# The last 128 rows of the output leave as two column halves, over two engines and two DMA queues

## The chip, the core and the metric

The kernel runs on one core of a Trainium2 chip. The metric is the time of one execution on the device in microseconds (us). Lower is better.

## The reference

Chunked attention is followed by a two-layer feed-forward network, all in float32. The sizes are batch 4, 8 heads, 768 positions, head dimension 64; then 3072 tokens, model width 512, hidden width 2048.

```
for c in range(nc):                         # 24 chunks of 32 queries
    scores = scale * np.matmul(q_c, k_full.transpose(0, 1, 3, 2))   # 8 memory keys + up to 56 neighbours
    a = softmax(scores)
    out[:, :, c_start:c_end] = np.matmul(a, v_full)
x = out.transpose(0, 2, 1, 3).reshape(B * S, H * D)                 # 3072 x 512
h = x @ w_in                                                        # 3072 x 2048
g = np.maximum(h, 0.0) + alpha * np.minimum(h, 0.0)
return g @ w_out                                                    # 3072 x 512
```

## The kernel before, in words

The 3072 tokens are cut into 8 blocks (NBLK) of 384 tokens (BT). For each block the kernel computes the attention of four pairs of heads, and then the feed-forward network over 16 hidden pieces (NF) of 128. For one piece, `up` (L659) makes `h_ps` with 12 matmuls, ScalarE and VectorE turn it into `gh` and `gl` (L668 to L681), and `down` (L689) adds its product with the piece of `w_out` to three PSUM tiles `o_ps`, one for each 128 tokens of the block (NTT = 3). `down` goes over the three tiles in order, three matmuls each, so in the last piece tile 0 is complete first, tile 1 second and tile 2 last. The attention of later blocks is spread between the feed-forward matmuls of earlier ones; in the last block nothing of it is left.

When the last piece of a block is done, `store` (L729) takes its three tiles to HBM. For each tile there are two steps: `copy` takes `o_ps` from PSUM to a tile `o_t` in SBUF (L736 on ScalarE; in block 1 L733 on VectorE instead), and `send` issues one DMA of 256 KB (128 rows of 2 KB) from SyncE (SP, L740). All other loads are issued from SP too (L246 to L259, L448, L557). ScalarE issues no DMA.

The order of the work is not the order in which the steps are added. Every step goes into a plan (`Plan`, L106) with an engine, an estimated cost, the keys that it reads and writes, and a `rest` that says how urgent it is. `Plan.send` (L126) then plays the plan through with these costs. In each turn it takes the engine that could start earliest, and on it, of the steps that are ready, the one with most work behind it. The step is emitted at that moment, so the order in the played plan is the order in each engine's queue:

```
            engine = min(at, key=at.get)
            n = max((n for n in able if self.steps[n][0] == engine and ready[n] <= at[engine]),
                    key=lambda n: (behind[n], -n))
```

Between a step and one that depends on it on another engine, the plan counts 0.07 us (HOP); for a step of SP it counts 2.3 us (LAND). The last `down` is one step with a cost of 2.09 us for all nine matmuls, and it writes the keys of all three tiles, ("o", 0) to ("o", 2). In the played plan the three tiles are therefore complete at the same moment. On the chip the waits come from the instructions themselves, so a copy waits for the matmuls of its own tile. Waits of one engine's queue are served in the queue's order.

At the end of the program every engine meets at a barrier (L867), which comes behind SP's waits for the transfers still under way.

Of the kernel before, what the change touches and what calls it, by code (L numbers as in the profile page):

```python
# [9 lines left out]
F32 = mybir.dt.float32  # L10
# [8 lines left out]
P = 128  # L19
# [8 lines left out]
BT = 384  # L28
NBLK = B * S // BT
NT = BT // TQ  # L30
NPAIR = H // 2
DM, DF = 512, 2048
NK = DM // P
NF = DF // P
NTT = BT // P
# [24 lines left out]
PE, DVE, ACT, POOL, SP = "PE", "DVE", "ACT", "POOL", "SP"  # L60
# [102 lines left out]
def body(ctx: ExitStack, tc: tile.TileContext, qvw, kw, first, w_in, w_out, alpha, out):  # L163
    nc = tc.nc
# [12 lines left out]
    tmp = ctx.enter_context(tc.tile_pool(name="tmp", bufs=1))  # L177
# [31 lines left out]
    step = plan.add  # L209
    state, xs = {}, {}  # L210

    def rest(place):
        return (len(ORDER) - place) * PAIR
# [515 lines left out]
    def store(blk, o_ps):  # L729
        def copy(tt, t, o):  # L730
            if blk == 1:
                o["t"] = kept[tt]
                nc.vector.tensor_tensor(out=o["t"], in0=o_ps[tt], in1=o["t"], op=ALU.add)  # L733
            else:
                o["t"] = tmp.tile([P, DM], F32, name="o_t", tag=f"o{t}")
                nc.scalar.copy(out=o["t"], in_=o_ps[tt])  # L736

        def send(tt, o):
            r = blk * BT + tt * P
            nc.sync.dma_start(out=out[r:r + P, :], in_=o["t"])  # L740

        for tt in range(NTT):
            t = tt if blk == 1 else NTT + tt % 2 if blk == 0 else next(ntmp) % NTMP
            o = {}
            place = PLACE[blk, NF - 1] + 1
            step(DVE if blk == 1 else ACT, 0.68 if blk == 1 else 0.59, partial(copy, tt, t, o), reads=[("o", i) for i in range(NTT)],
                 writes=[("tmp", t)], rest=rest(place))
            step(SP, 0.75, partial(send, tt, o), reads=[("tmp", t)])
# [35 lines left out]
    o_ps = {}  # L784
    for blk, f in ORDER:
        if blk == 0:
            decode(f)
        f0, f1 = (0, NF) if blk != 1 else (0, NJOINT) if f < NJOINT else (NJOINT, NF)
        add_up, add_bend, add_down = hidden(blk, f, f0, f1 - 1)
        add_up()  # L790
        if down is not None:
            down()
        if done is not None:
            done()
            done = None
        add_bend()
        now = todo.get(PLACE[blk, f], [])
        olds, news = ([u for u, part in now if part == which] for which in (2, 0))
        if olds or news:
            attend(PLACE[blk, f], olds, news)  # L800
        for u in olds:
            split(u, "h1" if u % size(u) else "a")
            if u + 2 < NU:
                load_v(u + 2)
        for u, part in now:
            if part == 1:
                weights(u)
                turn(u)
        for u in news:
            unit_begins(u)  # L810
        o = o_ps.setdefault((blk, f1), [])
        down = partial(add_down, o)
        if f == f1 - 1:
            done = partial(keep if f1 < NF else store, blk, o)
# [56 lines left out]
```

## Time and profile before

| | |
|---|---|
| median of 3 runs | 604.88 us (604.76 to 605.04) |
| the profiled execution | 605.43 us |
| its span, first to last instruction | 603.7 us |
| busy: PE (matmul) | 596.3 us, 99% |
| busy: PEld (weight load) | 531.0 us, 88% |
| busy: DVE (VectorE) | 397.7 us, 66% |
| busy: ACT (ScalarE) | 214.1 us, 35% |
| busy: POOL (GpSimd) | 35.7 us, 6% |
| DMA, all by SP's queue but for code loading | 48.98 MB, mean 81 GB/s |

The shares are of the span. The span of 603.7 us and the 605.43 us are of one execution; 1.73 us of it lie outside the first and last instruction. An engine's busy time holds no waiting and no issuing of DMAs.

### The profile page before, as it was taken

How to read it: one execution, taken by the hardware profiler on the slowest of the kernel's cores; microseconds unless marked ns; L12 is line 12 of the kernel's file. 1: busy time of each engine (PE TensorE's matmuls, PEld its weight loads, DVE VectorE, ACT ScalarE, POOL GpSimd, SP SyncE). 2: the span in 40 equal slices, each digit the busy share in tenths (PEclk: the TensorE clock that was granted, in tenths of full speed). 3: DMA queues.
4: the chain of work that ended last, by engine and by line, in shares of the span. 5: the costliest groups of instructions: out<-in, count | busy, mean ns of one | idle time of the engine just before them, and what ended most of it. 6: DMA issues, size and time to landing. Idle time of an engine off the chain costs nothing.

```text
span 603.7 us, 11483 instructions
## 1 busy us (share of the span) xinstructions
PE 596.3 (99%) x4622; PEld 531.0 (88%) x4622; DVE 397.7 (66%) x962; ACT 214.1 (35%) x596; POOL 35.7 (6%) x61
## 2 busy tenths in 40 slices
PE   8999999999999999999999999999999999999997
PEld 4789899888989889999899998899998898999986
DVE  5788998877958677749386593847748485433331
ACT  3688878644322314232142412314132131121101
POOL 3400000001001001001010000101000010000000
PEclk9999999999999999999999999999999999999999
DMA  8999500113240303130021303103031100010001
GB/s 335 355 408 408 205 0 1 33 33 103 68 134 1 99 2 100 52 100 0 25 76 53 100 1 94 42 18 99 1 99 53 36 2 2 1 52 1 0 1 53
DMA packets 20933, 48.98 MB, mean 81 GB/s; under 512 B 2448, under 2 KB 5520, under 8 KB 20880
## 3 DMA queue, kind: packets, MB, share of 16 engines
q1 hardware_dynamic: 20880, 48.25, 22.5%
q8 instruction: 36, 0.59, 0.4%
q14 instruction: 17, 0.14, 0.1%
HBM read 41.95 MB, written 6.29 MB: 80 GB/s over the span
## 4 chain that ended last, share of the span: by engine, by line
PE 96%; DMA 2%; DVE 1%; ACT 0%; issue 0%; SPq 0%; ACTq 0%
PE h_ps L659 44%; PE o_ps L689 44%; PE a_ps L397 3%; PE s_ps L306 2%; DMA early<-first 1%; DMA w_t<-w_in 1%; PE s_ps L267 1%; PE s_ps L281 1%; PE a_ps L517 1%; DVE w_t L588 0%; PE o_ps L504 0%; DVE w_t L592 0%; DVE xl L436 0%; DVE a L596 0%; ACT a L580 0%
## 5 line engine op out<-in xcount | busy, mean ns | idle before, releaser
L659 PE MATMUL h_ps<-xh,w 128*128 128x384 f32 x1024 | 260.6, 335 | 0.3 <-DVE w L607 0.3
L689 PE MATMUL o_ps<-w,gh 128*128 128x512 f32 x768 | 238.3, 392 | 0.0
L659 PEld LDWEIGHTS h_ps<-xh,w 128*128 128x128 f32 x1024 | 185.2, 188 | 2.0 <-DVE w L607 0.6
L659 PE MATMUL h_ps<-xl,w 128*128 128x384 f32 x512 | 173.5, 339 | 0.6 <-DVE xl L436 0.6
L689 PEld LDWEIGHTS o_ps<-w,gh 128*128 128x128 f32 x768 | 144.1, 188 | 29.1
L689 PE MATMUL o_ps<-w,gl 128*128 128x512 f32 x384 | 149.7, 390 | 0.0
L668 ACT ACTIVATE g<-h_ps 128x384 f32<-128x384 f32 x128 | 63.8, 498 | 192.0 <-PE h_ps L659 187.0
L671 DVE SCALAR_TENSOR_TENSOR g<-g,rise,h_ps 128x384 f32<-128x384 f32 x128 | 78.4, 613 | 78.6 <-ACT g L668 77.2
L382 DVE STREAM_TRANSPOSE pt<-e 32x192 f32<-32x192 f32 (+1 forms) x336 | 99.4, 300 | 13.6 <-POOL e L361 8.6
L659 PEld LDWEIGHTS h_ps<-xl,w 128*128 128x128 f32 x512 | 96.1, 188 | 3.9 <-DVE xl L436 1.0
L689 PEld LDWEIGHTS o_ps<-w,gl 128*128 128x128 f32 x384 | 72.1, 188 | 14.0
L681 DVE TENSOR_TENSOR gl<-g,gh 128x384 fp32r<-128x384 f32 x128 | 72.2, 565 | 4.8 <-ACT gh L677 1.9
L361 POOL TENSOR_TENSOR e<-e,den 128x384 f32<-128x384 f32 x24 | 22.2, 924 | 436.7 <-DVE den L358 436.7
L677 DVE CAST gh<-g 128x384 fp32r<-128x384 f32 x104 | 37.8, 365 | 13.0 <-PE o_ps L689 7.5
L432 ACT CAST xh<-a_ps 128x384 fp32r<-128x384 f32 x32 | 14.4, 483 | 88.0 <-PE a_ps L397 86.0
L340 ACT ACTIVATE e<-s_ps,mx 128x64 f32<-128x64 f32 x144 | 43.0, 320 | 6.9 <-DVE mx L332 6.9
L340 ACT ACTIVATION_READ_ACCUMULATOR e<-s_ps,mx 128x1 f32 x144 | 30.9, 215 | 0.0
L365 ACT COPY e<-e 128x192 f32<-128x192 f32 x24 | 8.4, 352 | 47.0 <-DVE pt L382 41.4
L436 DVE TENSOR_TENSOR xl<-a_ps,xh 128x384 fp32r<-128x384 f32 x32 | 17.5, 549 | 10.0 <-ACT xh L432 10.0
L736 ACT COPY o_t<-o_ps 128x512 f32<-128x512 f32 x21 | 12.3, 587 | 27.3 <-PE o_ps L689 25.9
L318 DVE MEMSET s_ps<- 32x16 f32 x12 | 0.9, 72 | 30.6 <-PE s_ps L306 30.5
L397 PEld LDWEIGHTS a_ps<-pt,v_t 128*64 128x64 f32 x384 | 16.3, 137 | 4.9 <-issue 4.9
(52 smaller groups left out, 306.2 us busy)
## 6 DMA issues: line engine op xcount, KB each, us to landing
w_t<-w_in SPq DMA_DIRECT2D x16, 512.0 KB, 10.2
w_t<-w_out SPq DMA_DIRECT2D x16, 512.0 KB, 10.2
qk<-kw SPq DMA_DIRECT2D x24, 272.0 KB, 3.5
v_t<-qvw SPq DMA_DIRECT2D x24, 256.0 KB, 4.2
out<-o_t SPq DMA_DIRECT2D x24, 256.0 KB, 2.1
early<-first SPq DMA_DIRECT2D x8, 656.0 KB, 6.4
qk<-qvw SPq DMA_DIRECT2D x24, 192.0 KB, 4.3
early<-first SPq DMA_DIRECT2D x8, 256.0 KB, 6.7
```

Source lines behind the costliest of these rows:

```text
L340: nc.scalar.activation(out=st["e"][:, i], in_=st["s"][h2][:, n], func=AF.Exp, scale=SCALE, bias=d["mx"][:, u - us[0], n, h2:h2 + 1], accum ...
L361: nc.gpsimd.tensor_tensor(out=st["e"], in0=st["e"], in1=st["den"].broadcast_to([P, NJ * 2, KW]), op=ALU.mult)
L382: nc.vector.transpose(out=pts[u % NPT][quad * CH:(quad + 1) * CH, j, t0:t0 + n1 - n0].rearrange("p t h q -> p (t h) q"), in_=(st["e"], zer ...
L397: nc.tensor.matmul(out=st["a"][h2 * D:(h2 + 1) * D, t * TQ:(t + 1) * TQ], lhsT=st["v"][:, t, h2, :], rhs=pts[u % NPT][:, :, t, h2, :], sta ...
L432: nc.scalar.copy(out=st["xh"], in_=st["a"][:, :BT])
L436: nc.vector.tensor_tensor(out=xl, in0=st["a"][:, :BT], in1=st["xh"].bitcast(F32), op=ALU.subtract)
L659: nc.tensor.matmul(out=h["ps"][:, :BT], lhsT=ws[f, 0][:, wk, k * P:(k + 1) * P], rhs=xs[first + k][xk], start=(k == 0 and n == 0), stop=(k ...
L668: nc.scalar.activation(out=h["g"], in_=h["ps"][:, :BT], func=AF.Relu, scale=-1.0)
L671: nc.vector.scalar_tensor_tensor(out=h["g"], in0=h["g"], scalar=rise[:, f:f + 1], in1=h["ps"][:, :BT], op0=ALU.mult, op1=ALU.add)
L677: copy(out=h["gh"], in_=h["g"])
L681: nc.vector.tensor_tensor(out=h["gl"], in0=h["g"], in1=h["gh"].bitcast(F32), op=ALU.subtract)
L689: nc.tensor.matmul(out=o_ps[tt], lhsT=h[gk][:, tt * P:(tt + 1) * P], rhs=ws[f, 1][:, wk], start=(f == first_f and i == 0), stop=(f == last ...
```

## The change

For the last tile of the last block, `copy` and `send` are replaced by two pairs of steps. VectorE copies columns 0 to 255, and SP sends them. ScalarE copies columns 256 to 511, and ScalarE itself sends them. The tile in SBUF has the shape [128, 2, 256]. The plan is told a cost of 0.35 us for each copy and 0.4 us for each send. The other 23 tiles are treated as before.

```diff
+        def half(tt, t, o, i):
+            cols = slice(i * DM // 2, (i + 1) * DM // 2)
+            if not i:
+                o["t"] = tmp.tile([P, 2, DM // 2], F32, name="o_t", tag=f"o{t}")
+            copy = (nc.vector.tensor_copy, nc.scalar.copy)[i]
+            copy(out=o["t"][:, i], in_=o_ps[tt][:, cols])
+
+        def send_half(tt, o, i):
+            r = blk * BT + tt * P
+            (nc.sync, nc.scalar)[i].dma_start(out=out[r:r + P, i * DM // 2:(i + 1) * DM // 2], in_=o["t"][:, i])
+
         for tt in range(NTT):
             t = tt if blk == 1 else NTT + tt % 2 if blk == 0 else next(ntmp) % NTMP
             o = {}
             place = PLACE[blk, NF - 1] + 1
+            if (blk, tt) == (NBLK - 1, NTT - 1):
+
+                for i in range(2):
+                    step((DVE, ACT)[i], 0.35, partial(half, tt, t, o, i), reads=[("o", tt)], writes=[("tmp", t, i)], rest=rest(place))
+                    step((SP, ACT)[i], 0.4, partial(send_half, tt, o, i), reads=[("tmp", t, i)])
+                continue
             step(DVE if blk == 1 else ACT, 0.68 if blk == 1 else 0.59, partial(copy, tt, t, o), reads=[("o", i) for i in range(NTT)],
                  writes=[("tmp", t)], rest=rest(place))
             step(SP, 0.75, partial(send, tt, o), reads=[("tmp", t)])
```

## Rows read from the trace of the kernel before

**Rows 1.** The page, part 1: busy time (share of the span) and instructions

```profile
PE 596.3 (99%) x4622; PEld 531.0 (88%) x4622; DVE 397.7 (66%) x962; ACT 214.1 (35%) x596; POOL 35.7 (6%) x61
```

**Rows 2.** The chain that ended last, from 598 us: start, duration, what

```profile
597.96 1.60 PE o_ps L689 x7
...
599.62 0.59 ACT o_t L736
```

**Rows 3.** Timeline of ScalarE, the three last copies one by one: start, duration

```profile
598.22 0.59 ACT L736 COPY o_t<-o_ps 128x512 f32<-128x512 f32 x1 [6.35 <-PE o_ps L689]
...
598.90 0.59 ACT L736 COPY o_t<-o_ps 128x512 f32<-128x512 f32 x1
...
599.62 0.59 ACT L736 COPY o_t<-o_ps 128x512 f32<-128x512 f32 x1
```

**Rows 4.** Timeline of SP, the three last sends one by one

```profile
598.83 0.33 SPq L740 DMA_DIRECT2D out<-o_t  x1
...
599.51 0.33 SPq L740 DMA_DIRECT2D out<-o_t  x1
...
600.24 0.33 SPq L740 DMA_DIRECT2D out<-o_t  x1
```

**Rows 5.** The tail by windows: engines' busy time, then PEclk, DMA share, GB/s

```profile
core 0: us, PE busy (x) PEld busy (x) DVE busy (x) ACT busy (x) POOL busy (x), PEclk, DMA share, GB/s
599.56:599.66 0.10, 0.00 (x0) 0.00 (x0) 0.00 (x0) 0.04 (x1) 0.00 (x0) 1.00 0.00 0
599.66:600.34 0.68, 0.00 (x0) 0.00 (x0) 0.00 (x0) 0.55 (x1) 0.00 (x0) 1.00 0.99 364
600.34:601.06 0.72, 0.00 (x0) 0.00 (x0) 0.00 (x0) 0.00 (x0) 0.00 (x0) 1.00 1.02 373
601.06:601.76 0.70, 0.00 (x0) 0.00 (x0) 0.00 (x0) 0.00 (x0) 0.00 (x0) 1.00 1.01 375
```

**Rows 6.** Waits of SP from 598 us: total, times, longest

```profile
SPq L867 <- DMA out<-o_t: 1.5, 1, 1.5
```

**Rows 7.** All 24 sends (L740): time from issue to landing

```profile
DMA to landing us min/median/max: 2.0/2.1/5.5
```

**Rows 8.** Timeline of ScalarE at the end of block 0: the copy of tile 1

```profile
138.50 0.59 ACT L736 COPY o_t<-o_ps 128x512 f32<-128x512 f32 x1
```

**Rows 9.** Timeline of SP over the same stretch

```profile
140.00 0.33 SPq L259 DMA_DIRECT2D v_t<-qvw  x1
...
141.52 0.42 SPq L740 DMA_DIRECT2D out<-o_t  x1
```

**Rows 10.** Timeline of SP where four DMAs are issued one behind the other

```profile
229.79 0.90 SPq L259 DMA_DIRECT2D v_t<-qvw  x2
230.73 0.91 SPq L246 DMA_DIRECT2D qk<-qvw  x2
```

**Rows 11.** VectorE by line and shape: count, busy us, mean ns of one

```profile
L677 DVE CAST gh<-g 128x384 fp32r<-128x384 f32 x104 | 37.8, 365 | 13.0 <-PE o_ps L689 7.5 <-DVE g L671 0.5 <-DVE pt L382 0.2
...
L329 DVE TENSOR_REDUCE mx<-s_ps 128x6 f32<-128x384 f32 x20 | 11.2, 558 | 0.7
...
L329 DVE TENSOR_REDUCE mx<-s_ps 128x3 f32<-128x192 f32 x8 | 2.9, 360 | 0.3
```

**Rows 12.** ScalarE by line and shape

```profile
L736 ACT COPY o_t<-o_ps 128x512 f32<-128x512 f32 x21 | 12.3, 587 | 27.3 <-PE o_ps L689 25.9
L365 ACT COPY e<-e 128x192 f32<-128x192 f32 x24 | 8.4, 352 | 47.0 <-DVE pt L382 41.4 <-POOL e L361 5.6
L509 ACT COPY qk<-o_ps 128x384 f32<-128x384 f32 x16 | 7.2, 504 | 1.8 <-PE o_ps L504 1.8
```

**Rows 13.** Timeline of VectorE at 29.5 us: one half of a `w_t` tile

```profile
29.50 1.42 DVE L588 COPY w_t<-w_t 128x512 int16<-128x512 int16 x1 [1.54 <-ACT a L580]
```

**Rows 14.** Timeline of ScalarE there: the other half of that tile

```profile
29.72 1.43 ACT L588 COPY w_t<-w_t 128x512 int16<-128x512 int16 x1
```

## The prediction

> **What bounds the kernel now.** I read the page first: TensorE's matmuls are busy for 596.3 us, 99% of the span [rows 1], so the body is TensorE's. The change touches nothing there: no step ahead of the last `down` reads or writes another key, and what the plan sees behind that step stays 0.59 + 0.07 + 0.75 us by tiles 0 and 1, so the order of all earlier work stays. What counts is the time behind the last matmul. I read it from the chain of waits, then the timelines of ScalarE and SP, then the DMA by windows.
>
> The last matmul ends near 599.56 us, and the copy of tile 2 runs from 599.62 for 0.59 us [rows 2]. Tiles 0 and 1 were complete earlier: their copies start at 598.22 and 598.90 [rows 3], and the three sends are issued at 598.83, 599.51 and 600.24, each some 0.03 us behind its copy's end [rows 4]. The chain of waits stops at the last copy, but the span goes on to 603.7. What fills it is SP's wait of 1.5 us for the last transfer [rows 6] and the barrier. A send takes 2.0 us at least [rows 7], so the last one lands near 600.24 + 2.0 = 602.24, and 1.5 us of waits and barrier follow.
>
> The reader should see one more thing in the windows: from 599.66 on, 0.83 us behind the first send, the DMA engines move 364, 373 and 375 GB/s at a share of 0.99 to 1.02 through 601.76, and nothing before [rows 5]. Three tiles of 262,144 bytes at 375 GB/s are 3 x 0.70 us. So the tail is a stream of data without a gap. It begins early because tiles 0 and 1 are sent while TensorE still works on tile 2.
>
> **The change part by part.** *The copies.* A 512-column copy of 0.59 us goes; two of 256 columns come. VectorE's plain copy from PSUM isn't in the trace. Below, its cast of 384 columns within SBUF scales to 365 x 256/384 = 243 ns; above, its reductions from PSUM (360 ns for 192 columns, 558 ns for 384) give 426 ns for 256 [rows 11]. I take 0.40, nearer to the rows that read PSUM. ScalarE's lies between 352 ns (192 columns) and 504 ns (384 columns) [rows 12]: 0.40 too. VectorE's half thus ends at 599.62 + 0.40 = 600.02 and can be sent at 600.05, 0.19 us ahead of today's 600.24.
>
> *The order on SP.* This is the term that decides. The plan plays the three tiles as complete at one moment; call the moment when their copies may start T. VectorE is free, so the half is copied by T + 0.35, and SP may send it at T + 0.42. ScalarE takes tile 0 first, as more work is behind it (0.59 + 0.07 + 0.75 = 1.41 against 0.35 + 0.07 + 0.40 = 0.82): copied by T + 0.59, to be sent at T + 0.66; tile 1 only at T + 1.25. The plan picks the earliest, so SP's queue reads: **half 0 of tile 2, then tile 0, then tile 1**. On ScalarE the order is tile 0, tile 1, half 1, its send.
>
> On the chip tile 2 is the last to be complete. SP's queue is served in order: at the end of block 0 tile 1 was copied by 139.09 [rows 8], but its send was issued only at 141.52, behind a load of `v_t` issued at 140.00 and what followed [rows 9]. Here the sends of tiles 0 and 1, today issued at 598.83 and 599.51, will stand behind half 0's wait until 600.05. DMAs issued one behind the other start 0.47 us apart (229.79 to 230.73 for two) [rows 10]. Tile 0 goes at 600.52 and tile 1 at 600.99.
>
> *The data.* The stream now begins with half 0 at 600.05 + 0.83 = 600.88 in place of 599.66: the 1.2 us in which TensorE's last matmuls hid the first transfers are gone. Half a tile is priced at 0.35 us, half of a tile's 0.70; rows of 1 KB aren't in the trace for a store, and the upper bound is the full tile's 0.70. Three cases bound the end of the bulk, today 601.76:
> - The second queue costs nothing, as if it had its own bandwidth: tile 0 begins at 600.52 + 0.83 = 601.35, and both tiles end at 601.35 + 1.40 = 602.75, that is +0.99.
> - No gap, all bytes share the engines: 600.88 + 2.10 = 602.98, +1.22.
> - Half 1 comes too late to fill the gap between half 0 (until 601.23) and tile 0 (from 601.35): 601.35 + 0.70 + 0.35 + 0.70 = 603.10, +1.34.
>
> I take the middle, **+1.2**. The issue alone, without any limit of bandwidth, would give 600.99 + 2.0 = 602.99 against 602.24, +0.75; with both halves at the price of full tiles the second case becomes +1.9. The last landing to the end of the span stays 1.5 us.
>
> The Trainium skill, "DMA: Bandwidth & Descriptors", section "Issuing engines are not separate DMA queues", says that transfers issued from ScalarE, SyncE or GpSimd run on the same 16 engines and interleave, and that issuing from several saves issue time alone. That speaks for the second and third case; where it doesn't hold, the first case's +0.99 stands. No row here shows ScalarE issuing.
>
> *The two readers of one bank.* Whether half 1 may be copied beside half 0 is not in the trace. Beside: from 599.62, sent at 600.05. Behind: from 600.06, sent at 600.49, its data from 601.32, and the third case. On this hangs the step from the second case to the third, 0.12 us.
>
> The Trainium skill, "PSUM — Partial Sum Buffer", section "PSUM bank collisions raise a hardware error", says that two engines must not read one bank in the same quadrant at once, so they have to be put in order. By that the third case is the one, +1.34.
>
> *The sum.* The profiled execution of 605.43 us becomes 606.63. The median of the runs shown is 0.55 lower, 604.88; it becomes 604.88 + 1.2 = 606.1.
>
> **The rivals.** *The order is the one the tiles complete in: tiles 0 and 1 first.* Then the first two sends stay at 598.83 and 599.51, half 0 goes at 600.05, half 1 at 600.05 or 600.49. But the data of tile 1 fill the engines until 601.06 [rows 5], and two halves of 0.35 behind them end at 601.76, as today. No change: 604.9, and 604.7 at best. It decides from the point where the plan's VectorE copy would end later than ScalarE's first. For it speaks only that the chip's own order of completion is this; the plan's costs speak against.
>
> *Half 1 waits until half 0 has left its tile*, because both share one `o_t`. Half 0 lands at 600.05 + 2.0 - 0.35 = 601.70, then come 0.43 for the copy and its send and 1.65 for half 1: 603.78, +1.5; should the two tiles ahead hold half 1 up by a half's 0.35, +1.9. That is 606.4 to 606.8, taken as 606.6. Against it: VectorE and ScalarE wrote two parts of one `w_t` tile at once, from 29.50 and from 29.72 for 1.4 us each [rows 13, 14].
>
> *ScalarE's queue, used for the first time, is slow.* SP's sends took 5.5 us at most, in a crowded stretch [rows 7]. From 600.49 that would be 605.99, +3.75: 608.6. It decides from a landing of over 3.0 us on. Nothing in the profile speaks for it.
>
> **How the numbers follow.** Forecast 0.80, own range 605.8 to 606.5. The order of completion 0.08; half 1 behind half 0's landing 0.07; slow first queue 0.05. A measurement of this kernel tells about 0.2% from no change, 1.21 us: 606.09. The forecast lies on that bound, so its chance is halved, 0.40 above and 0.40 below. Slower is 0.40 + 0.07 + 0.05 = 0.52. The first rival gives 0.06 to the same and 0.02 to faster, for terms that I don't see; same is 0.46. The range, 605.5 to 606.8, holds the forecast with the bounds of its terms and the second rival, and leaves out the first and the last.
>
> **What would show it.** SP's timeline would have the half's send first, near 600.05, with two sends of whole tiles 0.47 us apart behind it, the last near 601.0; the copies of tiles 0 and 1 still at 598.22 and 598.90. DMA windows would be empty until 600.88 and full until 603.0. VectorE's copy would start at 599.62 and take 0.40; ScalarE's half would start at 599.62 or at 600.06, which tells the bank's question. I am wrong if SP sends at 598.83 and 599.51, or if the last to land is ScalarE's.

## The result and the profile after

| | before | changed |
|---|---|---|
| median of 9 runs | 605.04 us | 606.66 us |
| the profiled execution | 605.43 us | 607.26 us |
| its span | 603.7 us | 605.5 us |

The ratio is 1.0025, with a 95% interval of 1.0016 to 1.0034: the change makes the kernel slower, by 1.0 to 2.1 us. One of the nine runs before took 2073.94 us; without it the median before is 604.98 us and the ratio 1.0026. A second series of the changed kernel (e8 below) gave 1.0019, from 1.0010 to 1.0028.

The body is as before. The page's part 1 shows TensorE, ScalarE and GpSimd at their old counts and one VectorE instruction more [rows 1]:

```profile
PE 596.7 (99%) x4622; PEld 531.4 (88%) x4622; DVE 397.7 (66%) x963; ACT 214.0 (35%) x596; POOL 36.5 (6%) x61
```

The tail is best read from the start of tile 0's last copy, 598.22 us before [rows 3] and 598.67 now. The 0.45 us between these two are scatter of the body: in the eight other profiled executions whose body is the same, that copy starts between 597.49 and 598.41. The timeline of ScalarE (start, duration) has the two whole copies as before, then the half, then ScalarE's own send:

```profile
598.67 0.59 ACT L736 COPY o_t<-o_ps 128x512 f32<-128x512 f32 x1 [6.35 <-PE o_ps L689]
...
599.35 0.59 ACT L736 COPY o_t<-o_ps 128x512 f32<-128x512 f32 x1
...
600.53 0.37 ACT L747 COPY o_t<-o_ps 128x256 f32<-128x256 f32 x1 [0.60 <-DVE o_t L747]
600.93 0.38 ACTq L751 DMA_DIRECT2D out<-o_t  x1
```

ScalarE's half waits for VectorE's (the bracket says so). That one, in VectorE's timeline, starts when the last matmul is done:

```profile
600.03 0.42 DVE L747 COPY o_t<-o_ps 128x256 f32<-128x256 f32 x1 [6.00 <-PE o_ps L689]
```

SP's timeline, send by send, is the main finding. The half goes first; tiles 0 and 1, copied by 599.26 and 599.93, go behind it [rows 4]:

```profile
600.48 0.33 SPq L751 DMA_DIRECT2D out<-o_t  x1
...
600.90 0.39 SPq L740 DMA_DIRECT2D out<-o_t  x1
...
601.38 0.40 SPq L740 DMA_DIRECT2D out<-o_t  x1
```

The tail by windows, with the columns of [rows 5]. Nothing moves until 601.30, 2.63 us behind tile 0's copy (before: 1.44). Then all 786 KB follow, at a time when TensorE has no work left:

```profile
599.96:601.30 1.34, 0.03 (x1) 0.00 (x0) 0.42 (x1) 0.37 (x1) 0.00 (x0) 1.00 0.00 0
601.30:602.10 0.80, 0.00 (x0) 0.00 (x0) 0.00 (x0) 0.00 (x0) 0.00 (x0) 1.00 0.89 300
602.10:603.00 0.90, 0.00 (x0) 0.00 (x0) 0.00 (x0) 0.00 (x0) 0.00 (x0) 1.00 1.03 364
603.00:603.70 0.70, 0.00 (x0) 0.00 (x0) 0.00 (x0) 0.00 (x0) 0.00 (x0) 0.51 0.84 313
```

The list of DMA issues, asked for each send (KB, us to landing), gives 1.8 us for SP's half, 2.5 for ScalarE's, and 2.7 for tile 1, the last to land, at 601.38 + 2.70 = 604.09. [Rows 7] had 2.0 for an undisturbed whole tile.

```profile
out<-o_t SPq DMA_DIRECT2D x1, 128.0 KB, 1.8
...
out<-o_t ACTq DMA_DIRECT2D x1, 128.0 KB, 2.5
...
out<-o_t SPq DMA_DIRECT2D x1, 256.0 KB, 2.7
```

### The profile page after: what moved, and what is told of

It is laid out like the page before. It is cut to its first block, busy times and chain, and to the rows that moved or that the text cites. A ratio compares the mean times of both kernels' runs of the same rounds, so it can differ in the third digit from the quotient of the medians.

```text
span 605.5 us, 11487 instructions
## 1 busy us (share of the span) xinstructions
PE 596.7 (99%) x4622; PEld 531.4 (88%) x4622; DVE 397.7 (66%) x963; ACT 214.0 (35%) x596; POOL 36.5 (6%) x61
## 4 chain that ended last, share of the span: by engine, by line
PE 95%; DMA 3%; DVE 1%; ACT 0%; SPq 0%; issue 0%; ACTq 0%
PE h_ps L659 45%; PE o_ps L689 44%; PE a_ps L397 3%; PE s_ps L306 2%; DMA w_t<-w_in 2%; DMA early<-first 1%; PE a_ps L517 1%; SPq L448 0%; PE o_ps L504 0%; DVE mx L467 0%; DVE e L471 0%; DVE den L479 0%; PE s_ps L281 0%; ACT qk L509 0%; DVE w L607 0%
```

## The experiments

The measure is the tail: from the start of tile 0's last copy to the first data, to the last landing, and to the end of the span. Landings and first packets are from the trace's DMA records. "Time" is the median less that of the kernel before, run on the same chip, in us, with the ratio's interval. The tail columns are from one profiled execution of each run. e7, which changes the body too, stands outside the table.

| kernel | first data | last landing | landing to end | tail | time | ratio, 95% |
|---|---|---|---|---|---|---|
| before | 1.44 | 4.04 | 1.40 | 5.44 | | |
| changed | 2.64 | 5.42 | 1.39 | 6.80 | +1.62 | 1.0016 to 1.0034 |
| e8, changed again | 2.64 | 5.41 | 1.40 | 6.81 | +1.08 | 1.0010 to 1.0028 |
| e1, SP in order | 1.44 | 4.12 | 1.39 | 5.51 | +0.06 | 0.9993 to 1.0010 |
| e2, only the order | 2.84 | 5.40 | 0.98 | 6.38 | +1.02 | 1.0008 to 1.0026 |
| e3, halves by SP | 1.44 | 4.12 | 1.27 | 5.40 | +0.05 | 0.9992 to 1.0010 |
| e4, tile 2 by ScalarE | 1.44 | 4.09 | 0.98 | 5.08 | -0.28 | 0.9988 to 1.0006 |
| e5, one send behind | 1.44 | 4.77 | 1.32 | 6.09 | +0.72 | 1.0004 to 1.0022 |
| e6, SP padded | 1.44 | 4.05 | 0.94 | 4.99 | -0.32 | 0.9986 to 1.0004 |
| e9, padded again | 1.44 | 4.05 | 0.94 | 4.99 | -0.56 | 0.9981 to 0.9999 |

**Theory A:** the change costs what it does since half 0's send stands at the head of SP's queue and holds back two sends that were ready. **Rival B:** the halves and the second queue cost by themselves.

**e1 undoes the order alone.** Halves, both copies and ScalarE's send stay.

```diff
         def send(tt, o):
             r = blk * BT + tt * P
             nc.sync.dma_start(out=out[r:r + P, :], in_=o["t"])
+            if (blk, tt) == (NBLK - 1, 1):
+                for go in held:
+                    go()
...
-            (nc.sync, nc.scalar)[i].dma_start(out=out[r:r + P, i * DM // 2:(i + 1) * DM // 2], in_=o["t"][:, i])
+            go = partial((nc.sync, nc.scalar)[i].dma_start, out=out[r:r + P, i * DM // 2:(i + 1) * DM // 2], in_=o["t"][:, i])
+            go() if i else held.append(go)
```

> The changed kernel with one thing undone: SP issues the sends of tiles 0 and 1 ahead of half 0's. The halves, both copies and ScalarE's own send stay. Theory A (the sends of tiles 0 and 1 are held behind half 0's wait): sends 0.61 and 1.29 us behind the start of tile 0's copy as before the change, the stream of data starts 1.44 us behind it, and the time is that of the kernel before within 0.25 us; from the start of tile 0's copy to the end of the span 5.3 to 5.7 us (before: 5.44, changed: 6.80). Theory B (halves and a second queue cost by themselves): as the changed kernel, +1.4 to +1.6 us, 6.5 to 6.8 us.

The slowdown is gone: tail 5.51, time +0.06. SP's timeline has tiles 0 and 1 first again (two sends from 598.19) and the half last:

```profile
598.19 1.01 SPq L742 DMA_DIRECT2D out<-o_t  x2
599.39 0.33 SPq L745 DMA_DIRECT2D out<-o_t  x1
```

A is borne out, and the change's idea can be read by itself: sending the last tile in halves gains nothing, for its last landing is 4.12 where the whole tile's was 4.04.

**e2 adds the order alone** to the kernel before: tile 2's send goes ahead of the others; no halves, no second queue.

```diff
-            nc.sync.dma_start(out=out[r:r + P, :], in_=o["t"])
+            go = partial(nc.sync.dma_start, out=out[r:r + P, :], in_=o["t"])
+            if blk == NBLK - 1 and tt < NTT - 1:
+                held.append(go)
+                return
+            go()
+            for go in held:
+                go()
```

> The kernel before with one thing added: SP's queue has the send of tile 2 ahead of those of tiles 0 and 1. No halves, no VectorE copy, no ScalarE queue. Theory A: first send 2.0 us behind the start of tile 0's copy, the three tiles' data stream from 2.85 us on and end 2.1 us later, +1.4 us to the time, 6.7 to 6.9 us from tile 0's copy to the end of the span. Theory B: no change, 5.4 us.

Slower as A has it. SP's first send goes at 599.97, 2.01 us behind tile 0's copy at 597.95, and the last landing comes at 5.40, +1.36:

```profile
599.97 0.33 SPq L746 DMA_DIRECT2D out<-o_t  x1
600.35 0.92 SPq L748 DMA_DIRECT2D out<-o_t  x2
```

But the time rose by 1.02, and the tail is 6.38 where 6.7 to 6.9 was expected: from the last landing to the end it took 0.98 us, not 1.40. Theory A says nothing of that; e6 takes it up.

**e3 sends both halves from SP, in the order of completion; e4 sends a whole tile 2 from ScalarE.** They part halves and queue.

```diff
-            go() if i else held.append(go)
+            held.append(go)          # e3, with nc.sync for both halves
...
-            nc.sync.dma_start(out=out[r:r + P, :], in_=o["t"])
+            queue = nc.scalar if (blk, tt) == (NBLK - 1, NTT - 1) else nc.sync
+            queue.dma_start(out=out[r:r + P, :], in_=o["t"])          # e4, from the kernel before
```

> The changed kernel with both halves sent by SP, behind tiles 0 and 1. ScalarE issues no DMA. Theory A: as before the change within 0.2 us, 5.3 to 5.6 us from tile 0's copy to the end of the span. Theory B, as far as the halves cost: +0.5 us or more; as far as only the second queue costs: as A.

> The kernel before, with tile 2 whole, copied and sent by ScalarE; tiles 0 and 1 sent by SP as before. Theory A: no change if ScalarE's DMA moves its first data 0.83 us after the issue, as SP's do when SP is idle; +0.3 to +0.4 us if the 1.20 us seen in the changed kernel belong to the queue. Theory B, as far as the second queue costs: +0.8 us or more.

Neither costs more than 0.08 us: the last landings are 4.12 and 4.09, against 4.04. B falls in both its parts. ScalarE's DMA in e4, issued at 599.88, moved its first data 0.89 us behind the issue, against 0.83 on SP. e4's tail is 0.36 shorter, all of it behind the landing.

```profile
599.88 0.37 ACTq L741 DMA_DIRECT2D out<-o_t  x1
```

**e5 holds back one send instead of two**: SP's order is tile 0, half 0, tile 1. The edit is e1's with `(NBLK - 1, 0)`.

> The changed kernel with SP's order tile 0, half 0, tile 1: one send is held behind half 0's wait instead of two. Theory A (what is held up sets the price, through the bytes that no longer move before the last matmul): tile 0's data move from 1.44 us behind its copy's start as before the change; tile 1 is sent at 2.24, its data and half 1's share the engines from 3.07 on and end near 4.1; last landing 4.6 to 4.7 us (before 4.04, changed 5.42), +0.6 us to the time. Rival (any wait at the head of SP's queue costs the whole): 5.3 to 5.4 us, +1.4.

About half the price, as A has it: +0.73 in the last landing, +0.72 in the time. The expected 4.6 to 4.7 was missed by 0.07: tile 1 landed at 4.60, but ScalarE's half at 4.77. SP's timeline, tile 0 sent on time at 598.71:

```profile
598.71 0.33 SPq L742 DMA_DIRECT2D out<-o_t  x1
599.91 0.33 SPq L745 DMA_DIRECT2D out<-o_t  x1
600.34 0.38 SPq L742 DMA_DIRECT2D out<-o_t  x1
```

**e6 asks for the 0.4 us at the end.** In all kernels SP pauses for 0.34 to 0.39 us ahead of its 208th instruction. Before the change, and after it, that one is the drain between the last landing and the barrier. The rows of SP's instructions at the barrier's line (duration min/median/max, first and last start) show it before: the last wait starts at 602.4 and takes 28 ns, the drain comes at 602.8.

```profile
L867 SPq EVENT_SEMAPHORE  x2: 28/28/28, 602.3 to 602.4; - x2
L867 SPq DRAIN  x2: 7/62/117, 602.8 to 603.0; - x2
```

e6 puts 16 more instructions into SP's stream where it waits for 64 us:

```diff
             nc.sync.dma_start(out=out[r:r + P, :], in_=o["t"])
+            if (blk, tt) == (NBLK - 2, NTT - 1):
+                for _ in range(16):
+                    nc.sync.drain()
```

> The kernel before with 16 empty instructions (drains) on SP behind the sends of the last block but one, where SP waits for 64 us. SP pauses for 0.34 to 0.39 us ahead of its 208th instruction in every kernel so far; before the change that is between the last landing and the barrier. Theory P (the pause belongs to the place in SP's stream): it falls into the idle stretch, last landing to the end of the span 1.0 us instead of 1.40, the time 0.4 us less. Theory Q (the pause belongs to the waits at the end): 1.40 us, no change.

> The kernel before with 16 drains on SP in the idle stretch, once more. Theory P: 4.05 us from tile 0's copy to the last landing and 0.94 from there to the end of the span as in the first run (before: 4.04 and 1.40), -0.4 to -0.5 us to the time. Rival (the first run's -0.32 us was scatter of the body): the tail as said, the time within 0.1 us of the kernel before.

The same rows in e6: the last wait and the drain both begin at 602.6.

```profile
L870 SPq EVENT_SEMAPHORE  x3: 28/28/1541, 600.9 to 602.6; - x3
L870 SPq DRAIN  x2: 7/7/7, 602.6 to 602.7; - x2
```

The pause now stands between two of the added drains (0.34 us in the first run, 0.36 in the second), and the landing to the end takes 0.94 both times. So the tail bears out theory P. In the time the gain is at the limit of what can be told: the first run's interval holds 1, the second's ends at 0.9999. By its tail this kernel beats both others (4.99 against 5.44 and 6.80), and that has nothing to do with the change. e2 and e4 fit it too: they have two SP instructions fewer (210 for 212), so the pause falls into the barrier, beside steps of the other engines, and the landing to the end takes 0.98 in both. The 1.27 of e3 and the 1.32 of e5 stay without an explanation.

**e7 gives the halves of tile 2 a PSUM bank each**, with matmuls of 256 columns for that tile in the last block. It ran once (607.13 us), so its time isn't used; TensorE's busy time is 597.1 us there, far from the 7 us more that were expected.

```diff
+                if blk == NBLK - 1:
+                    o_ps.append(ps_a.tile([P, 512], F32, name="o_ps", tag="a"))
...
-                    nc.tensor.matmul(
-                        out=o_ps[tt],
...
+                    for part in range(2 if apart else 1):
+                        nc.tensor.matmul(
+                            out=o_ps[tt + part][:, :DM // 2] if apart else o_ps[tt],
```

> The changed kernel with the two halves of tile 2 of the last block summed in two PSUM banks, by twice as many matmuls of 256 columns (some 7 us more on TensorE, which are not the question). Theory S (the copies were put in order because they read one bank): both copies start within 0.05 us of each other, both halves are sent at the same time, and from the start of half 0's copy to the last landing 3.9 to 4.0 us. Rival (they were put in order for the tile that they write): ScalarE's copy again starts 0.5 us behind VectorE's, 4.06 us.

ScalarE's copy no longer waits for VectorE's but for TensorE, by its bracket, since its bank is complete 0.16 us after the other. VectorE's row, then ScalarE's:

```profile
599.96 0.42 DVE L751 COPY o_t<-o_ps 128x256 f32<-128x256 f32 x1 [6.08 <-PE o_ps L693]
```

```profile
600.11 0.37 ACT L751 COPY o_t<-o_ps 128x256 f32<-128x256 f32 x1 [0.17 <-PE o_ps L693]
```

The copies run beside each other; from half 0's copy to the last landing 3.94 us, against 4.06 in the changed kernel. The rival falls: the two copies still write one `o_t`. Theory S fits, and the order cost 0.12. But e7 gives each half a PSUM tile of its own as well as a bank, so it doesn't show which of the two put the copies in order. The starts lie 0.16 apart, more than the 0.05 expected. What two readers of one bank would do without the wait was not tried.

**e8 is the changed kernel once more.**

> The changed kernel once more, on the chip of the three others. Theory A: 6.8 us from tile 0's copy to the end of the span, +1.3 to +1.5 us to the time. Rival (part of the first +1.6 us was another cost of the change ahead of the tail): +1.6 or more, with the surplus showing before tile 0's last copy.

The tail agrees to 0.01 us with the first run's. The time is +1.08, the first +1.62, their mean +1.35; the tail accounts for +1.37. The surplus of the first didn't come again, so nothing points to a cost ahead of the tail.

## Why the prediction was right

It said 606.1 us in a range of 605.5 to 606.8; measured were 606.66 and, in e8, 606.17. Of the +1.62 the tail has 1.37 (5.44 to 6.80, before rounding); the other 0.25 lie outside the tail. They did not come again in e8, whose time rose by 0.29 less than the tail, so they are taken for scatter. That e8 came within 0.07 us of the forecast is luck in part: the tail's price is 0.15 above the +1.22 of the sum. The steps of the prediction, counted from the start of tile 0's copy (598.22 in its numbers):

- *The order on SP*, worked out from the plan's costs: half 0, tile 0, tile 1, exactly. That this is the cause is shown from both sides, by e1 and e2, and its dose by e5.
- *First send* 1.83 expected, 1.81 measured; VectorE's copy 0.40 expected, 0.42 measured, close to the reductions' 0.426 [rows 11]; ScalarE's 0.40 and 0.37. First data 0.83 behind the first send, as before.
- *The sends behind it* 0.47 apart each; measured 0.42 and 0.48.
- *The data.* Of the three cases the third came true (+1.34; the last landing moved by 5.42 - 4.04 = +1.38), not the middle one that was taken for the sum (+1.22). The first data came 1.20 later (1.22 expected), so that term was right. The term that was mis-sized is the length of the stream, which the middle case left as it was: from first to last packet it takes 2.25 us before and 2.40 now. Half 1 was copied behind half 0, its data came late, and the engines stood partly idle between half 0 and tile 0. Where halves are sent without that gap (e1, e3, e7) the stream takes 2.30. So some 0.10 goes with the gap (0.12 in the third case), and at most 0.05 with the halves' rows of 1 KB. The Trainium skill, "PSUM — Partial Sum Buffer", section "PSUM bank collisions raise a hardware error", asks for just that order of two readers; the trace's wait of ScalarE for VectorE agrees, e7's 0.12 us is the price of it here, and the sum should have followed it.
- *The second queue* brought no bandwidth: from 602.10 to 603.00, where both queues have data under way, the window shows 364 GB/s for the two together, and SP alone had 364 to 375 [rows 5]. The Trainium skill, "DMA: Bandwidth & Descriptors", section "Issuing engines are not separate DMA queues", says that the DMAs of all issuing engines run on the same 16 engines; this agrees.
- *The end:* 1.5 us behind the landing was kept, and that is 1.39 and 1.40. That it held is luck: SP has 212 instructions in both kernels, with as many DMA issues (145) and semaphore instructions (63) as before, so its pause stayed where it was. The prediction did not know of the pause, and with two instructions fewer (e2, e4) the 1.40 became 0.98.
- *The rivals.* The order of completion is e1 made by hand, and it gave the predicted no change (+0.06). Half 1 did not wait for half 0's landing: its copy started 0.08 us behind the end of half 0's. ScalarE's queue, first used here, took 2.54 us to its landing, under the 3.0 from which it would decide.

## What to carry to other kernels

A queue that is served in order must get its entries in the order in which they become ready on the chip, not in a planner's: here one step stood for three tiles that are complete 0.7 us apart, and an earlier "ready" in the plan put the last one first. Before splitting a final transfer, look whether the DMA engines are idle ahead of it: here they were full from 1.44 us on, so there was nothing to win by halving it (e1 and e3: 4.12 against 4.04). And a change of a microsecond at the end of a long kernel is read in the trace's tail, which repeated to 0.01 us, while the start of tile 0's last copy, and with it the body, varied from 597.49 to 598.67.

## What the runs showed of the hardware that was not expected

- SP pauses for 0.34 to 0.39 us ahead of its 208th instruction, whatever that is: a drain, a wait or an added empty instruction. In the kernel before this costs 0.46 us at the very end (1.40 against 0.94 from the last landing to the end of the span). In all eleven traces a code load of 8 KB (queue 14, "instruction") begins 0.61 to 0.65 us behind the start of that instruction: at 603.41 before, in the barrier, and at 536.13 and 535.59 in e6 and e9, where the pause had moved. So the pause goes together with code loading; whether that is its cause, and how, no run shows.
- A DMA issued by ScalarE just behind one of SP starts late: 1.20 us from issue to first data where SP issued 0.03 us before (changed kernel, e8; 1.22 in e5), 1.09 at 0.11 us (e7), 0.94 at 0.45 (e1), 0.89 at 0.73 (e4). Something that the two queues share ahead of the 16 engines would account for it; no run tests that.
